# Weight loads, weight stores and phase loads issued in another order in a fused S4D and GLU kernel

## Chip, cores and metric

The kernel runs on one core of a Trainium2 chip. The metric is device time in microseconds (us). Beside the times there is one profiled execution of the kernel; its trace lists every instruction on the engines PE (TensorE), with PEld for its weight loads, DVE (VectorE), ACT (ScalarE), POOL (GpSimd) and SP (SyncE), which here does nothing but issue DMAs ("SPq" in the views).

## The reference

For a sequence of 2048 positions with D = 448 channels, the sum of three terms over a layer-normalised input:

```python
def _A_ref(u, log_A_real, A_imag, C_real, C_imag, log_dt, D_skip):
    ...
    P = jnp.exp((A * dt[:, None])[:, :, None] * pos[None, None, :])
    K = 2.0 * jnp.einsum("dn,dnl->dl", C, P).real
    ...
    y = jnp.fft.irfft(Uf * Kf[None, :, :], L2)[:, :, :L]
    ...
    return y + u * D_skip[None, None, :]
...
def _B_ref(x, w_gate, w_up, w_down):
    g = jnp.einsum("bsd,df->bsf", x, w_gate)
    u = jnp.einsum("bsd,df->bsf", x, w_up)
    h = _sigmoid(g) * u
    return jnp.einsum("bsf,fd->bsd", h, w_down)
...
return x + _A_ref(xn, ...) + _B_ref(xn, w_gate, w_up, w_down)
```

A is a long convolution whose kernel K is made of 256 complex exponentials a channel; B is a gated linear unit with F = 1792 inner columns.

## The kernel before

Everything is fp32, done on PE as products of split numbers: each operand is cast to fp32r (the high part) and the rest is kept as a low part, and a product is high x high + high x low + low x high.

**The GLU** (`glu()`) runs over two halves of the positions. In each half it takes 14 tiles of 128 inner columns, in groups of 3, 3, 3, 3 and 2. For a tile it gets wh and wl (high and low of w_gate and w_up; two buffers each), runs two gates (`gate`, the matmuls of line 687 into gu, then th on ACT, hf on DVE, and the split of hf into hh on ACT and hl on DVE), and gets dh and dl (high and low of w_down). After a group come the down products (line 794, po) and their sums on DVE (line 799, acc). In half 0 the raw weights are loaded by `w_load` (lines 621 and 623: per matrix one transfer of 192 KB and two of 32 KB, into wraw, one buffer) and `rd_load` (line 629), and split: wh on ACT (line 737), wl on DVE (line 741), dh on ACT (line 762), dl on POOL (line 763). Tiles 3 and 6 to 13 are not split again in half 1: wh, wl, dh and dl are stored to DRAM (wt_d at line 744, dt_d at line 766) right after they are made and read back in half 1 (line 752, 775). The loads of tiles 0 and 1 are issued at the start of the program.

**The convolution's kernel.** A preparation splits phases U, V and T of all channels into high and low parts and stores them to ph_d in DRAM (12 stores at lines 384 and 389). `kgen` then goes over 56 chunks of 8 channels. For each pair of chunks `phase_load` (line 470) brings the rows of ph_d into a tile ph (two of them) in nine transfers of 8 rows. For a chunk, PE multiplies ph with the constant sel (line 520, tr), ACT turns that into sines and cosines (S, lines 528 to 531), POOL raises magnitudes me and mf by products of powers pm (line 498), which DVE (line 435) and ACT (lines 433 and 438) made every eighth chunk in `powers`, DVE multiplies them (Et at lines 581 and 582, Ft at line 583), and PE forms 64 products a chunk in ko (line 595). Every fourth chunk ACT copies ko to ks (line 608) and PE takes it through the first stage of a Fourier transform (line 546, kp and kq). After the last chunk come spectra and inverse transforms.

**The order.** `glu` and `kgen` are generators; each `yield` tells how much PE work was issued, and a driver alternates between them by that. A scheduler then arranges the instructions of each engine once, when the program is built; on the chip each engine, and SP, works strictly in its own order, and a waiting instruction holds everything behind it on that engine. `tc.issue_after(x)` keeps an instruction behind x in that order, `hp` raises its priority.

Of the kernel before, what the change touches and what calls it, by code (L numbers as in the profile page):

```python
# [11 lines left out]
F32 = mybir.dt.float32  # L12
F32R = mybir.dt.float32r
I32 = mybir.dt.int32
AF = mybir.ActivationFunctionType
ALU = mybir.AluOpType
# [4 lines left out]
D = 448  # L21
N = 256
# [6 lines left out]
NFT = F // 128  # L29
# [9 lines left out]
CP = D // 4  # L39
# [8 lines left out]
DC = 8  # L48
# [7 lines left out]
def _tables():  # L56

    a = np.arange(NA)[:, None]
    k1 = np.arange(NK1)[None, :]
    ang = 2 * np.pi * ((a * k1) % 64) / 64.0  # L60


    wk = np.zeros((4, NA, 2, 2, 32))

    wx = np.zeros((4, NA, 64))
    for j in range(4):
        wk[j, :, 0, j % 2] = np.cos(ang)[:, :32]
        wk[j, :, 1, j % 2] = -np.sin(ang)[:, :32]
        wk[j, :, 1, j % 2, 0] = np.cos(ang)[:, 32]
        wx[j, :, :NK1] = np.cos(ang)  # L70
        wx[j, :, NK1:] = -np.sin(ang)[:, 1:32]
    b = np.arange(NB)[:, None]
    k2 = np.arange(64)[None, :]
    tab = np.zeros((NK1, 128, 128))
    bk = np.zeros((2, 2, 64, 2, 128))
    for q in range(NK1):
        al = 2 * np.pi * ((b * (q + 64 * k2)) % 4096) / 4096.0
        c, s = np.cos(al), np.sin(al)
        tab[q] = np.block([[c, -s], [s, c]])
        if q in (0, 32):  # L80


            for h in range(2):

                split = lambda t: t.reshape(64, 2, 32).transpose(0, 2, 1)
                both = lambda r, i: np.stack([split(r), split(i)], 3).reshape(64, 128)
                bk[q // 32, h, :, 0] = both(c.T, s.T)
                bk[q // 32, h, :, 1] = both(-s.T, c.T)

    tab[0, 64:] = 0.0  # L90
    t32 = np.concatenate([tab[32][:, None], bk[1].reshape(128, 2, 128)], 1)
    tab = tab[:32].reshape(8, 4, 128, 128).transpose(0, 2, 1, 3)

    wf = np.zeros((2, 2, 4, 8, 32, NA))
    for k in range(32):
        ang = 2 * np.pi * ((k * (64 * np.arange(NA)[None] + np.arange(64)[:, None])) % 4096) / 4096.0
        re = (1.0 if k == 0 else 2.0) / 4096.0 * np.cos(ang)
        im = -2.0 / 4096.0 * np.sin(ang)
        if k == 0:
            im = np.broadcast_to(np.cos(np.pi * np.arange(NA))[None] / 4096.0, im.shape)  # L100
        wf[:, 0, k % 4, k // 4] = re.reshape(2, 32, NA)
        wf[:, 1, k % 4, k // 4] = im.reshape(2, 32, NA)

    sel = np.zeros((128, 2, DC, 32))
    st = np.arange(32) + 0.5
    for e in range(DC):
        sel[[e, DC + 2 + e, 2 * DC + 2 + e], 0, e] = st, -st, -st  # L110
        sel[[64 + e, 66 + 2 * DC + e, 96 + e], 1, e] = st, -st, -st
        sel[[64 + DC + e, 96 + DC + e, 96 + 2 * DC + e], 1, e] = [[1.0], [-1.0], [-1.0]]
    for row, tb_ in ((DC, 0), (64 + 2 * DC, 1)):
        sel[row, tb_], sel[row + 1, tb_] = MAGIC, -MAGIC
    f = lambda v, s: np.ascontiguousarray(v.reshape(s).astype(np.float32))
    return {
        "c_wk": f(wk, (128, 2, 64)),
        "c_wx": f(wx, (128, 64)),
        "c_tab": f(tab, (8, 128, 4, 128)),
        "c_t32": f(t32, (128, 3, 128)),  # L120
        "c_bk": f(bk[0], (128, 2, 128)),
        "c_wf": f(wf, (128, 32, NA)),
        "c_sel": f(sel, (128, 512)),
        "c_id": np.eye(128, dtype=np.float32),
    }
# [3 lines left out]
def s4d_glu_kernel(ctx, tc, io):  # L129
    nc = tc.nc  # L130
# [5 lines left out]

    dram = ctx.enter_context(tc.tile_pool(name="dram", bufs=1, space=DRAM))
    acc_d = dram.tile([128, 8, D], F32, name="acc_d")
    ph_d = dram.tile([D, 6, N], F32, name="ph_d")
    x1_d = dram.tile([64, NB, D], F32, name="x1_d")  # L140
    sk_d = dram.tile([128, D // 32, 32, 32], F32, name="sk_d")
    wt_d = dram.tile([2, NFT, 128, 8 * 128], F32, name="wt_d")
# [188 lines left out]
    def prep(pool, h, srcs):  # L331
# [44 lines left out]
            v.tensor_scalar(part(fr, i), part(aim, i), 1.0 / TWO_PI, dt(i), ALU.mult, ALU.mult)  # L376
        nc.scalar.copy(ki, fr)
        U, V, T = aim, fr, w3
        rows = ph_d[2 * CP * h : 2 * CP * h + 2 * CP].rearrange("(t p) i n -> p t i n", t=2)

        def high(i, src):
            hi = slots[f"P{i}"][:, h]
            nc.scalar.copy(hi, src)
            nc.sync.dma_start(rows[:, :, 2 * i], three(hi).bitcast(F32))

        def low(i, src):
            lo = src.bitcast(F32R)
            nc.gpsimd.tensor_tensor(lo, src, slots[f"P{i}"][:, h], ALU.subtract)
            nc.sync.dma_start(rows[:, :, 2 * i + 1], three(lo).bitcast(F32))

        v.tensor_tensor(U, fr, ki, ALU.subtract)
        nc.scalar.activation(ki, U, AF.Identity, scale=64.0)
# [32 lines left out]
                ps[:, :, :CP].rearrange("p k (g e) -> p k g e", e=DC),  # L425
            )

    def powers(pms, g, behind=None):

        w = W1s[0][:, NCH * g : NCH * g + NCH].rearrange("p g h e -> p (g h e)")  # L430
        pm = pms[g % 2]
        with tc.issue_after(behind.ins) if behind else nullcontext():
            nc.scalar.activation(pm[:, 0], w, AF.Identity, bias=one)
        for j in (1, 2, 3, 4, 5, 7, 8, 9, 10, 11):
            v.scalar_tensor_tensor(pm[:, j], w, 2.0, w, ALU.add, ALU.mult)  # L435
            w = pm[:, j]
        for o in (slice(1, 6), slice(7, 12)):
            nc.scalar.activation(pm[:, o], pm[:, o], AF.Identity, bias=one)

    def kgen(pk):  # L440
        fts, mls, sins = [], [], []
# [13 lines left out]
        pms = [tl["pm0"]]  # L455
        nc.gpsimd.memset(pms[0][:, 6], 1.0)
        with hp(HP):
            powers(pms, 0)


        pht = [tl["ph0"], tl["ph1"]]
# [2 lines left out]

        def phase_load(b):
            t = pht[b % 2]
            src = ph_d[16 * b : 16 * b + 16].rearrange("(k r) c n -> c r k n", k=2)
            for r0, parts in ((0, [0]), (DC + 2, [0, 1]), (64, [2, 4]), (66 + 2 * DC, [2]), (96, [3, 4, 5])):
                for j, i in enumerate(parts):
                    nc.sync.dma_start(t[r0 + DC * j : r0 + DC * j + DC].bitcast(F32), src[i])  # L470

        mes = [tl["me0"], tl["me1"]]
        nc.gpsimd.memset(mes[0][:, :, 0:1], 1.0)
# [91 lines left out]
        for g in range(NCK // NCH):  # L565
            for c in range(NCH):
# [1 line left out]
                S = nxt  # L568
                me, mf = (m[:, 2 * DC * (c % 2) : 2 * DC * (c % 2) + 2 * DC] for m in mags)
                if c == 4 and NCH * (g + 1) < NCK:  # L570
                    with tc.issue_after(fts[0].ins):
                        powers(pms, g + 1, sins[0])
                if cn + 1 < NCK:
                    nxt = ahead(cn + 1)
                    if c % 2 == 1:
# [39 lines left out]
    def w_load(f, raw=None, eng=nc.sync):  # L615
        fs = slice(128 * f, 128 * f + 128)
        if raw is None:
            raw = pg.tile([128, 2, 4, 128], F32, name="wraw", bufs=1)
        for i, nm in enumerate(("B_w_gate", "B_w_up")):
            w = io[nm]  # L620
            eng.dma_start(raw[:, i, 0:3], w[0:384, fs].rearrange("(k p) f -> p k f", p=128))
            for h in range(2):
                eng.dma_start(raw[64 * h : 64 * h + 64, i, 3], w[384:448, fs])
        return raw
# [81 lines left out]
        to.append((hh, hl))  # L706

    def glu():
        for half in range(2):
            if half == 1:  # L710
                for q in (2, 3):
# [2 lines left out]
            for fs_ in ORDER[half]:  # L714
# [14 lines left out]
                for n_, (f, t) in enumerate(order):  # L729
                    if t == 0:  # L730
                        wh = pg.tile([128, 2, 4, 128], F32R, name="wh", bufs=2)
                        if half == 0:
                            first = len(raws) == 2
                            raw, rd = raws.pop() if raws else (w_load(f), None)
                            wl = w_low()
                            with hp(HP):
                                nc.scalar.copy(wh, raw)
                                if first:
                                    v.scalar_tensor_tensor(wl, raw, lim[:, 0, 0:1], wh, ALU.mult, ALU.subtract)
                                else:  # L740
                                    v.tensor_tensor(wl, raw, wh, ALU.subtract)  # L741
                            if f not in RAW:
                                for t_, d_ in kept((wh, wl), wt_d, f):
                                    nc.sync.dma_start(d_, t_)
                        elif f in RAW:
                            raw, wl = w_load(f, eng=nc.gpsimd), w_low()
                            nc.gpsimd.tensor_copy(wh, raw)
                            nc.gpsimd.tensor_tensor(wl, raw, wh, ALU.subtract)
                        else:
                            wl = w_low()  # L750
                            for t_, d_ in kept((wh, wl), wt_d, f):
                                nc.sync.dma_start(t_, d_)
                        ws.append((wh, wl))
                    between = (lambda s_=mid[n_]: step(*s_)) if cross and mid[n_] else None
                    yield from gate(ws[f - f0], xq[2 * half + t], hs[t], between)
                    if t == 0:
                        dh = pg.tile([128, D], F32R, name="dh", bufs=FCH[0])
                        if half == 0:
# [3 lines left out]
                                nc.scalar.copy(dh, rd)  # L762
                            nc.gpsimd.tensor_tensor(dl, rd, dh, ALU.subtract)  # L763
                            if f not in RAW:
                                for t_, d_ in kept((dh, dl), dt_d, f):
                                    nc.sync.dma_start(d_, t_)
                        elif f in RAW:
                            dl = d_low()
                            rd = rd_load(f, pg.tile([128, D], F32, name="rdw", tag="wraw", bufs=1), nc.gpsimd)
# [360 lines left out]
```

## Time and profile before

| | us |
|---|---|
| runs | 749.53, 754.44, 755.01 (median 754.44) |
| profiled execution | 757.44 |
| its span, first to last instruction | 755.5 |
| mean granted TensorE clock over the span | 0.957 |

About 1.9 us of the profiled execution lie outside the span. In the timeline a row is the start and the duration in us, engine, line, operation with output and inputs, the number of like instructions in the row and, in brackets, how long the engine was idle before it and what ended that. A view of windows has one row a stretch: the busy time (and number) of each engine, the granted clock as a share of full speed, the share of DMA time and GB/s. The waits of SP list what a DMA issue waited for: us in total, how often, and the longest.

### The profile page before, as it was taken

How to read it: one execution, taken by the hardware profiler on the slowest of the kernel's cores; microseconds unless marked ns; L12 is line 12 of the kernel's file. 1: busy time of each engine (PE TensorE's matmuls, PEld its weight loads, DVE VectorE, ACT ScalarE, POOL GpSimd, SP SyncE). 2: the span in 40 equal slices, each digit the busy share in tenths (PEclk: the TensorE clock that was granted, in tenths of full speed). 3: DMA queues.
4: the chain of work that ended last, by engine and by line, in shares of the span. 5: the costliest groups of instructions: out<-in, count | busy, mean ns of one | idle time of the engine just before them, and what ended most of it. 6: DMA issues, size and time to landing. Idle time of an engine off the chain costs nothing.

```text
span 755.5 us, 19270 instructions
## 1 busy us (share of the span) xinstructions
PE 691.4 (92%) x7780; PEld 540.6 (72%) x7780; DVE 564.4 (75%) x776; ACT 421.5 (56%) x650; POOL 363.9 (48%) x423
## 2 busy tenths in 40 slices
PE   2798799995997999888999999999999999998994
PEld 2675588874886778555678887887877787776783
DVE  5769997697889889879558978988875555664553
ACT  3635455666777776987377777867742222322310
POOL 2102017695697668675328686596754001341001
PEclk9988899997999899989799999999999999999998
DMA  9926327434412543445663333222169999999646
GB/s 207 220 70 195 103 77 228 133 113 147 145 45 98 176 150 113 133 135 154 182 200 116 100 111 126 97 95 75 43 159 246 268 240 235 244 251 245 162 130 163
DMA packets 92776, 115.86 MB, mean 153 GB/s; under 512 B 12560, under 2 KB 80656, under 8 KB 92432
## 3 DMA queue, kind: packets, MB, share of 16 engines
q1 hardware_dynamic: 83376, 94.16, 45.7%
q10 hardware_dynamic: 6736, 14.57, 6.3%
q0 software_dynamic: 2576, 5.90, 3.2%
q8 instruction: 61, 1.00, 0.6%
q14 instruction: 27, 0.22, 0.1%
HBM read 70.75 MB, written 43.84 MB: 152 GB/s over the span
## 4 chain that ended last, share of the span: by engine, by line
PE 52%; DVE 14%; POOL 12%; DMA 8%; issue 5%; ACT 5%; SPq 2%; ACTq 1%; POOLq 0%; DVEq 0%
PE gu L687 20%; PE po L794 13%; PE sp L876 6%; POOL me L498 6%; PE ko L595 5%; PE pv L903 3%; POOL mf L498 3%; PE tr L520 2%; DVE Ft L583 2%; DVE Et L582 2%; DVE Et L581 2%; DVE wl L741 1%; POOL dl L763 1%; DVE pm L435 1%; DVE hl L705 1%
## 5 line engine op out<-in xcount | busy, mean ns | idle before, releaser
L498 POOL TENSOR_TENSOR me<-me,pm 128x32 f32<-128x32 f32 (+1 forms) x168 | 141.5, 842 | 101.4 <-DVE Et L582 89.8
L498 POOL TENSOR_TENSOR mf<-mf,pm 128x64 f32<-128x64 f32 (+1 forms) x112 | 118.5, 1058 | 4.2
L687 PE MATMUL gu<-xh,wh 128*128 128x512 f32 x336 | 103.3, 415 | 4.1 <-ACT xh L216 4.1
L687 PE MATMUL gu<-xh,wl 128*128 128x512 f32 x336 | 97.7, 398 | 0.0
L687 PE MATMUL gu<-xl,wh 128*128 128x512 f32 x336 | 96.3, 393 | 0.0
L794 PE MATMUL po<-dh,hh 128*128 128x448 f32 x224 | 86.5, 386 | 6.3 <-DVE acc L799 3.4
L581 DVE TENSOR_TENSOR Et<-me,S 128x1024 f32<-128x1024 f32 x56 | 77.7, 1388 | 14.8 <-ACT S L531 12.3
L582 DVE TENSOR_TENSOR Et<-me,S 128x1024 f32<-128x1024 f32 x56 | 78.8, 1408 | 13.3 <-ACT me L511 10.0
L794 PE MATMUL po<-dl,hh 128*128 128x448 f32 x224 | 84.0, 375 | 0.0
L794 PE MATMUL po<-dh,hl 128*128 128x448 f32 x224 | 83.5, 374 | 0.0
L583 DVE TENSOR_TENSOR Ft<-mf,S 128x1024 f32<-128x1024 f32 x56 | 78.4, 1400 | 4.4 <-POOL mf L498 3.1
L687 PEld LDWEIGHTS gu<-xh,wh 128*128 128x128 f32 x336 | 63.8, 197 | 23.2 <-ACT xh L216 5.6
L528 ACT ACTIVATE S<-tr 128x1024 f32<-128x1024 f32 x56 | 57.8, 1032 | 39.2 <-PE tr L520 37.5
L595 PEld LDWEIGHTS ko<-Et,Ft 128*32 128x32 f32 x3584 | 56.0, 113 | 30.4 <-issue 14.6
L703 ACT CAST hh<-hf 128x512 fp32r<-128x512 f32 x56 | 35.0, 625 | 75.6 <-DVE hf L698 64.8
L687 PEld LDWEIGHTS gu<-xh,wl 128*128 128x128 f32 x336 | 64.4, 192 | 15.5 <-DVE pl L304 0.7
L595 PE MATMUL ko<-Et,Ft 128*32 128x64 f32 x3584 | 66.6, 226 | 9.7 <-DVE Ft L583 5.3
L698 DVE SCALAR_TENSOR_TENSOR hf<-th,gu 128x512 f32<-128x512 f32 x56 | 38.2, 681 | 48.4 <-PE gu L687 37.0
L687 PEld LDWEIGHTS gu<-xl,wh 128*128 128x128 f32 x336 | 63.6, 189 | 14.2 <-issue 0.7
L799 DVE SCALAR_TENSOR_TENSOR acc<-po,acc 128x448 f32<-128x448 f32 x80 | 48.1, 615 | 25.8 <-PE po L794 25.7
L531 ACT ACTIVATE S<-S,hpi 128x1024 f32<-128x1024 f32 x56 | 65.6, 1172 | 0.0
L695 ACT ACTIVATE th<-gu 128x512 f32<-128x512 f32 x56 | 33.6, 600 | 55.9 <-PE gu L687 48.0
(196 smaller groups left out, 1308.4 us busy)
## 6 DMA issues: line engine op xcount, KB each, us to landing
sk_d<-sk ACTq DMA_DIRECT2D x14, 512.0 KB
sx<-x_d SPq DMA_DIRECT2D x32, 224.0 KB
skl<-sk_d SPq DMA_DIRECT2D x16, 448.0 KB
vp<-v_d SPq DMA_DIRECT2D x16, 448.0 KB
v_d<-vt SPq DMA_DIRECT2D x62, 112.0 KB
wt_d<-wh SPq DMA_DIRECT2D x9, 512.0 KB
wt_d<-wl SPq DMA_DIRECT2D x9, 512.0 KB
wl<-wt_d SPq DMA_DIRECT2D x9, 512.0 KB
```

The source lines that it names most:

```text
L498: ins = nc.gpsimd.tensor_tensor(m[:, :, w + a : 2 * w : n], m[:, :, a:w:n], par(base + i).unsqueeze(2).to_broadcast([128, 4 * DC, w // n]) ...
L528: nc.scalar.activation(rows(cs), pv, AF.Abs)
L531: sins[:] = [nc.scalar.activation(cs, cs, AF.Sin, scale=-TWO_PI, bias=hpi)]
L581: v.tensor_tensor(Et[:, :, :, 32:64], two(me[:, :, 32:64]), S[:, 1::-1], ALU.mult)
L582: v.tensor_tensor(Et[:, :, :, 0:32], two(me[:, :, 0:32]), S[:, 1:3, :, ::-1], ALU.mult)
L583: fts[:] = [v.tensor_tensor(Ft, two(mf), S[:, 3:5], ALU.mult)]
L595: mm = nc.tensor.matmul(ko[32 * j : 32 * j + 32, sl], Ft[:, cc, DC * h + 4 * q + j], Et[:, cc, DC * h + 4 * q + j], start=(k == 0), stop=( ...
L687: glu_mm[:] = [nc.tensor.matmul(ps, a_, b_, start=(n == 0), stop=(n == len(mm) - 1))]
L698: marks[1] = v.scalar_tensor_tensor(hf, th, 1.0, pgu[1], ALU.add, ALU.mult)
L794: glu_mm[:] = [nc.tensor.matmul(po, a_[:, bs], w_, start=(n == 0), stop=(n == 3 * fc - 1))]
L799: v.scalar_tensor_tensor(acc[:, b], po, 0.5, acc[:, b], ALU.mult, ALU.add)
L876: mm = nc.tensor.matmul(to, tb[:kk, t, 64 * c : 64 * c + 64], rhs, start=True, stop=True, skip_group_check=True,)
```

## The change

Four edits:

- In half 0 the raw weights of the next tile are loaded (`w_load(f + 1)`) right behind the instructions that make wl of this tile, ahead of its gates; before, they were loaded when the next tile's turn came. wraw keeps its one buffer.
- The stores of wh, wl, dh and dl go onto a list; the list is issued after the next gate.
- ph_d becomes three DRAM tiles: phu_d (high and low of U), phv_d (high V, high T, low T, low V) and phh_d (high V and high T a second time). A pair of chunks is loaded in four transfers of 8, 16, 16 and 32 rows; the rows of sel are permuted to match. The preparation issues 16 stores where it issued 12.
- `powers` becomes a generator in four pieces, which its callers run through at once; each piece stands behind the same Ft.

```diff
@@ tables @@
-        sel[[e, DC + 2 + e, 2 * DC + 2 + e], 0, e] = st, -st, -st
-        sel[[64 + e, 66 + 2 * DC + e, 96 + e], 1, e] = st, -st, -st
-        sel[[64 + DC + e, 96 + DC + e, 96 + 2 * DC + e], 1, e] = [[1.0], [-1.0], [-1.0]]
+        sel[[e, DC + 2 + 2 * e, DC + 3 + 2 * e], 0, e] = st, -st, -st
+        sel[[64 + 2 * e, 96 + 4 * e, 99 + 4 * e], 1, e] = st, -st, -st
+        sel[[65 + 2 * e, 97 + 4 * e, 98 + 4 * e], 1, e] = [[1.0], [-1.0], [-1.0]]
@@ preparation of the phases @@
-        rows = ph_d[2 * CP * h : 2 * CP * h + 2 * CP].rearrange("(t p) i n -> p t i n", t=2)
+        def keep(d, i, src):
+            rows = d[2 * CP * h : 2 * CP * h + 2 * CP].rearrange("(t p) i n -> p t i n", t=2)
+            nc.sync.dma_start(rows[:, :, i], three(src).bitcast(F32))

         def high(i, src):
             hi = slots[f"P{i}"][:, h]
             nc.scalar.copy(hi, src)
-            nc.sync.dma_start(rows[:, :, 2 * i], three(hi).bitcast(F32))
+            keep((phu_d, phv_d, phv_d)[i], (0, 0, 1)[i], hi)
+            if i:
+                keep(phh_d, i - 1, hi)

         def low(i, src):
             ...
-            nc.sync.dma_start(rows[:, :, 2 * i + 1], three(lo).bitcast(F32))
+            keep((phu_d, phv_d, phv_d)[i], (1, 3, 2)[i], lo)
@@ phase_load @@
-            src = ph_d[16 * b : 16 * b + 16].rearrange("(k r) c n -> c r k n", k=2)
-            for r0, parts in ((0, [0]), (DC + 2, [0, 1]), (64, [2, 4]), (66 + 2 * DC, [2]), (96, [3, 4, 5])):
-                for j, i in enumerate(parts):
-                    nc.sync.dma_start(t[r0 + DC * j : r0 + DC * j + DC].bitcast(F32), src[i])
+            for r0, d, n in ((0, phu_d, 1), (DC + 2, phu_d, 2), (64, phh_d, 2), (96, phv_d, 4)):
+                src = d[16 * b : 16 * b + 16, :n].rearrange("(k r) i n -> (r i) k n", k=2)
+                nc.sync.dma_start(t[r0 : r0 + DC * n].bitcast(F32), src)
@@ glu @@
-                            raw, rd = raws.pop() if raws else (w_load(f), None)
+                            raw, rd = raws.pop()
                             ...
+                            if not raws and f + 1 < NFT:
+                                raws.append((w_load(f + 1), None))
                             if f not in RAW:
-                                for t_, d_ in kept((wh, wl), wt_d, f):
-                                    nc.sync.dma_start(d_, t_)
+                                stores.extend(kept((wh, wl), wt_d, f))
                         ...
                     yield from gate(ws[f - f0], xq[2 * half + t], hs[t], between)
+                    for t_, d_ in stores:
+                        nc.sync.dma_start(d_, t_)
+                    stores.clear()
                     if t == 0:
                         ...
                             if f not in RAW:
-                                for t_, d_ in kept((dh, dl), dt_d, f):
-                                    nc.sync.dma_start(d_, t_)
+                                stores.extend(kept((dh, dl), dt_d, f))
```

In `powers` each of the four pieces is wrapped in `tc.issue_after(fts[0].ins)` and followed by a `yield`; before, the call as a whole was.

More of the change, by code (lines that the diff above doesn't have):

```diff
@@ L138, in s4d_glu_kernel @@
     acc_d = dram.tile([128, 8, D], F32, name="acc_d")
-    ph_d = dram.tile([D, 6, N], F32, name="ph_d")
+    phu_d = dram.tile([D, 2, N], F32, name="phu_d")
+    phv_d = dram.tile([D, 4, N], F32, name="phv_d")
+    phh_d = dram.tile([D, 2, N], F32, name="phh_d")
     x1_d = dram.tile([64, NB, D], F32, name="x1_d")
@@ L426, in turn, with powers @@
             )
-    def powers(pms, g, behind=None):
+    def powers(pms, g, fts, behind=None):
         w = W1s[0][:, NCH * g : NCH * g + NCH].rearrange("p g h e -> p (g h e)")
@@ L433, in powers @@
             nc.scalar.activation(pm[:, 0], w, AF.Identity, bias=one)
[L434 to L438, printed above, removed]
+        for js, o in (((1, 2, 3), None), ((4, 5, 7), slice(1, 6)), ((8, 9), None), ((10, 11), slice(7, 12))):
+            with tc.issue_after(fts[0].ins) if behind else nullcontext():
+                for j in js:
+                    v.scalar_tensor_tensor(pm[:, j], w, 2.0, w, ALU.add, ALU.mult)
+                    w = pm[:, j]
+                if o:
+                    nc.scalar.activation(pm[:, o], pm[:, o], AF.Identity, bias=one)
+            yield
     def kgen(pk):
@@ L457, in kgen @@
         with hp(HP):
-            powers(pms, 0)
+            for _ in powers(pms, 0, None):
+                pass
         pht = [tl["ph0"], tl["ph1"]]
@@ L570, in kgen @@
                 if c == 4 and NCH * (g + 1) < NCK:
-                    with tc.issue_after(fts[0].ins):
-                        powers(pms, g + 1, sins[0])
+                    for _ in powers(pms, g + 1, fts, sins[0]):
+                        pass
                 if cn + 1 < NCK:
@@ L708, in glu @@
     def glu():
+        stores = []
         for half in range(2):
```

## The prediction

> **What bounds the kernel now.** I read the page first (busy shares, slices, the chain of waits), then the idle gaps of PE one by one in the timeline, and the granted clock in 4 us windows around each.
>
> ```profile
> span 755.5 us, 19270 instructions
> ...
> PE 691.4 (92%) x7780; PEld 540.6 (72%) x7780; DVE 564.4 (75%) x776; ACT 421.5 (56%) x650; POOL 363.9 (48%) x423
> ...
> PE   2798799995997999888999999999999999998994
> ...
> PEclk9988899997999899989799999999999999999998
> ...
> PE 52%; DVE 14%; POOL 12%; DMA 8%; issue 5%; ACT 5%; SPq 2%; ACTq 1%; POOLq 0%; DVEq 0%
> ```
>
> The first three rows are the span, the busy time of each engine and PE in 40 slices of 18.9 us; then the clock granted to PE, and the shares of the chain that ended last. PE is busy for 691.4 of 755.5 us, so only 64 us are idle, and the rest can shrink only where matmuls ran at less than full clock. The change doesn't touch the number of matmuls. The slices lose time only in the left half: from about slice 21 (390 us) PE is at 9 throughout until the end. The changed edits work up to there (their phase loads go on to the last chunk), so what they are worth is read from the gaps before 390 us. SP, which issues nearly all DMAs and does most of what is edited, carries 2% of the chain.
>
> **The raw weights a tile ahead.** The largest early gap is this one.
>
> ```profile
> 31.78 1.19 PE L687 MATMUL gu<-xh,wh 128*128 128x512 f32 x4 [0.60 <-ACT xh L216]
> ...
> 32.80 0.60 PE L207 MATMUL tr<-ident,xn 128*128 128x128 f32 x4
> ...
> 34.17 0.38 SPq L621 DMA_DIRECT2D wraw<-in_B_w_up_dram  x1
> 35.11 1.10 SPq L623 DMA_DIRECT2D wraw<-in_B_w_up_dram  x2
> 35.57 0.56 ACT L762 CAST dh<-rd 128x448 fp32r<-128x448 f32 x1 [2.37 <-DMA rd<-in_B_w_down_dram]
> 36.04 0.58 ACT L216 CAST xh<-tr 128x512 fp32r<-128x512 f32 x1
> ...
> 36.31 1.41 SPq L629 DMA_DIRECT2D rd<-in_B_w_down_dram  x2
> 36.68 1.22 PE L687 MATMUL gu<-xh,wh 128*128 128x512 f32 x2 [3.27 <-ACT xh L216]
> ```
>
> Each timeline row is start, duration, engine, line, operation, and in brackets the idle time before it and what ended it. The transposes of x end at 32.80 + 0.60 = 33.40, but ACT stands in its queue at the cast of w_down, waiting for a DMA, and only then makes xh; PE waits 3.27 us. In the changed program's instruction order ACT casts xh ahead of this dh, because w_load of the next tile is now issued right behind wl and stands on SP ahead of rd; the cast of dh comes later. So PE waits only for the cast, as it did at 31.78, where the gap was 0.60: 3.27 - 0.60 = 2.7 us less idle. What is late next is dh of this tile; its DMA moves behind a raw load, whose rows here are issued in 0.38 + 1.10 us, so I let it land some 3 us later, at about 38.5 (35.57 + 3). Its cast then delays nothing until PE has finished its gate.
>
> The gap has a second price, the clock.
>
> ```profile
> 32.00:36.00 4.00, 1.40 (x8) 0.94 (x7) 3.94 (x7) 1.63 (x4) 0.00 (x0) 0.96 0.89 193
> 36.00:40.00 4.00, 3.32 (x8) 2.65 (x9) 3.96 (x16) 0.62 (x2) 1.14 (x1) 0.50 0.51 149
> ```
> ```profile
> 34.00:48.00 14.00, 11.32 (x38) 0.76 0.25 68
> ```
> ```profile
> 100.00:114.00 14.00, 13.85 (x61) 1.00 0.31 88
> ```
> ```profile
> 36.68 10.74 PE gu L687 x34
> ...
> 47.50 0.61 ACT th L695
> ...
> 48.13 0.07 DVE hf L698
> ```
>
> The first two windows have the busy time of PE, PEld, DVE, ACT and POOL, then the clock: 0.96 before the gap, 0.50 after it. The next two give the gate's matmuls (L687) alone: 38 in 11.32 us at clock 0.76, 0.298 each, against 13.85 / 61 = 0.227 at 1.00. The gap thus costs 38 x 0.071 = 2.7 us more, if it is what lowers the clock. For that speaks a later gap and the windows behind it:
>
> ```profile
> 358.24 0.47 PE L794 MATMUL po<-dh,hh 128*128 128x448 f32 x1 [2.21 <-DVE xl L214]
> ```
> ```profile
> 246.00:250.00 4.00, 4.00 (x106) 3.18 (x97) 3.88 (x4) 2.48 (x4) 1.78 (x1) 0.50 0.63 190
> ...
> 360.00:364.00 4.00, 4.00 (x43) 2.02 (x44) 2.97 (x5) 1.87 (x4) 0.00 (x0) 0.50 0.50 194
> ```
>
> After 2.21 us of idle time PE ran at 0.50, while the 0.60 us at 31.78 left the clock up. I take the clock term as gained, since 0.60 is far below 2.21, and its loss as a rival. The Trainium skill, in "TensorE: Matmul & The Clock Gate" (section "Part 1: The HAM clock gate"), lets the clock fall to half after about one idle window of some 3.4 us that runs freely; by that rule 3.27 us needn't lower it, something else may have, and the gain would be the idle time alone; the drop after 2.21 us doesn't agree with its figure.
>
> The chain of waits holds 34 of these matmuls, then th and hf; from then on DVE splits weights and prepares phases:
>
> ```profile
> 50.00:75.00 25.00, 22.14 (x108) 14.56 (x107) 24.74 (x41) 13.16 (x20) 4.08 (x1) 0.86 0.65 183
> ```
>
> It is busy for 24.74 of 25 us. A DVE without idle time moves as a whole: 2.7 + 2.7 = 5.4 us earlier. Its bounds are 0 (dh's cast, in order on ACT, holds the next th as long as it held xh) and 5.4.
>
> For later tiles the early call does little: raw has one buffer, so its load waits for wl of the tile before in both programs, and the order on SP shows these loads hoisted already.
>
> **The deferred stores, and the second large gap.**
>
> ```profile
> 171.21 1.20 POOL L763 TENSOR_TENSOR dl<-rd,dh 128x448 fp32r<-128x448 f32 x1
> ...
> 172.43 0.34 SPq L766 DMA_DIRECT2D dt_d<-dl  x1
> ...
> 174.63 1.66 SPq L623 DMA_DIRECT2D wraw<-in_B_w_up_dram  x2
> ...
> 178.01 1.04 ACT L737 CAST wh<-wraw 128x1024 fp32r<-128x1024 f32 x1 [5.95 <-DMA wraw<-in_B_w_up_dram]
> ...
> 182.81 0.56 ACT L608 COPY ks<-ko 128x512 f32<-128x512 f32 x1
> ...
> 183.42 0.37 PE L546 MATMUL kp<-wk,ks 64*64 64x64 f32 x1 [7.89 <-ACT ks L608]
> ```
> ```profile
> 184.00:188.00 4.00, 3.06 (x119) 2.90 (x112) 2.80 (x4) 4.00 (x6) 0.00 (x0) 0.50 0.37 109
> ```
>
> POOL delivers dl late, SP stands at its store with the rest of the next raw load queued behind it, ACT stands at wh waiting for that load, and ks, which PE needs, stands behind wh on ACT. The gap is 7.89 us, and at half clock the 3.06 us of the next window hold 1.5 us of excess. This is what deferring stores could cure. In the changed program's order, however, dl's store of this tile again comes before the second half of the raw load, POOL's order up to this dl is the same, and the nine phase loads before the store become four, while SP waits there anyway. So I cost the deferral at nothing here. Bounds: -9.4 (7.89 + 1.5) if the store does move out of the way, +1.4 if all of the later gate's stores wait: four at the 0.34 of the row.
>
> **The phases.** Preparing them issues 16 stores instead of 12, and the weight store passed by them moves; the rows of this place:
>
> ```profile
> 126.51 0.54 SPq L384 DMA_DIRECT2D ph_d<-P  x1
> ...
> 128.37 2.02 SPq L389 DMA_DIRECT2D ph_d<-w  x1
> ...
> 130.43 1.12 SPq L623 DMA_DIRECT2D wraw<-in_B_w_up_dram  x2
> ...
> 133.43 1.05 ACT L737 CAST wh<-wraw 128x1024 fp32r<-128x1024 f32 x1 [5.21 <-DMA ph<-ph_d]
> ```
>
> The last phase store stands ahead of a raw load on SP, and ACT waits for that at wh. Two of the four added stores come in this stretch, and 2 x 0.54 = 1.1 us is the upper bound, 0 the lower (the copies fit into SP's earlier waits); I take 0.8, as the last stores are the ones that count.
>
> ```profile
> 183.70 3.23 SPq L470 DMA_DIRECT2D ph<-ph_d  x9
> ```
> ```profile
> SPq L470 <- PE tr L520: 82.5, 16, 10.7
> ```
>
> The nine loads of a pair take SP 3.23 us, 0.36 each. Four instead of nine, in 28 pairs, is 140 x 0.36 = 50 us of SP. The second row says why this isn't 50 us of the kernel: SP waits 82.5 us in these loads for PE to release the tile, so they are mostly early. Only where a pair is late, as behind 128.37 above and at a few later pairs, are 5 x 0.36 = 1.8 us on the path; I take 0.8, about half of one such saving, between 0 and, for five late pairs, 5 x 1.8 = 9 us.
>
> powers keeps its instructions and its place behind the same Ft; DVE and ACT execute the same, at nothing.
>
> **The reordering.** The instructions of 195 to 390 us are arranged anew: the chunk work stands earlier against the gates (in the changed program PE comes to the twentieth chunk's ko after some 25 half-tiles of gate instead of 26). There PE now waits for products of DVE:
>
> ```profile
> 245.42 1.93 PE L595 MATMUL ko<-Et,Ft 128*32 128x64 f32 x64 [3.28 <-DVE Et L581]
> ```
>
> Transposes that come earlier feed ACT and DVE earlier, which helps; ko that comes earlier meets Et and Ft sooner, which hurts. Such a wait is 3.28 us and then, in the window from 246 shown above, 4.00 busy us at half clock, thus 2.0 more: 5.3. One of them more or less is the bound on my forecast; I take 0.
>
> Sum: -5.4 + 0.8 - 0.8 + 0 = -5.4 us. The profiled run took 757.44 us with a span of 755.5, 3.0 us (0.4%) over the median of 754.44; a difference of a few us carries over unscaled, so 754.4 - 5.4 = 749 us.
>
> **The rivals.** *Late weights cured as well.* The store leaves the way at 172 and the gap of 7.89 goes, or earlier transposes end one or two of DVE's waits: 749 - 9.4 = 740, with a wait of 5.3 more 734. For it: store and load stand in one queue, and both are moved. Against: POOL, not SP, is late at 171.21, and the order of the stores is the same.
>
> *The early gain is lost or halved.* If the clock falls at 36 us whatever the gap, only 2.7 us of idle time go: 752. If raw is not ahead (one buffer, a hoisted load) or dh holds ACT as before, nothing goes: 754. For it: ACT takes its work in order, and PE is idle elsewhere in its first two slices too (2 and 7 tenths busy). Against: the drop stands right behind the gap. The rule of the Trainium skill's "TensorE: Matmul & The Clock Gate" named above would give 752 here.
>
> *PE comes too early.* In order on PE, ko of chunks 12 to 25 moves ahead of gates that used to fill the time in which DVE and POOL make Et and Ft. Each chunk at which PE arrives more than some 2 us before the product costs 5.3; from the second on the early gain is gone; three make 749 + 16 = 765. For it:
>
> ```profile
> 225.00:250.00 25.00, 21.08 (x319) 16.71 (x317) 23.35 (x26) 17.69 (x27) 17.24 (x18) 0.88 0.32 107
> ```
>
> DVE has 23.35 of 25 us busy there, so it can't deliver sooner. Against: gates not done earlier remain to be done later, and PE's total is the same.
>
> **How the numbers follow.** Forecast 0.42, own range 744 to 754 (one wait of 5.3 either way); cured as well 0.27, 734 to 745; lost or halved 0.09, 752 to 755; PE too early 0.22, 757 to 770. About 1%, 7.5 us, is what a measurement here tells from no change. Faster than 746.9 are the second case and a quarter of the first: 0.27 + 0.10 = 0.37. Slower than 762 are four fifths of the last: 0.18. The rest is 0.45. The range leaves out the far ends of the second and the fourth case, about 0.1 each: 737 to 765.
>
> **What would show it.** In the new profile the gate near 34 us starts some 0.6 us after its transposes, with the clock at 1.00 until 44, and th follows at about 42 instead of 47.50; a gap over 2 us there, or half clock, refutes the first term. The wait of wh on the raw load and a gap of 7 to 8 us at ks should still stand near 173 to 178; if it is gone, the first rival holds. Phase loads appear as four issues of about 0.36. Waits before ko between 195 and 390 us should sum to what they are now within 5 us; three new ones over 2 us with windows at 0.50 make the slower rival right.

## The result, and the profile after

| | before | after |
|---|---|---|
| median of 15 runs, us | 754.45 | 748.48 |
| lowest and highest, us | 749.53, 761.67 | 743.47, 753.66 |
| profiled execution, span, us | 755.5 | 749.6 |
| its mean granted clock | 0.957 | 0.964 |

The ratio after to before is 0.9918 (95% interval 0.9889 to 0.9947): 6.2 us less. The ratios, here and below, leave out executions that took over 1.5% longer than the fastest of the same kernel, and the medians don't; the two differ where several are left out, four of twelve in e2 and four of eleven in e10. The forecast was 749, with 737 to 765 as its range, and the likeliest class, within 1%.

The page of the kernel after, the same rows as before:

```profile
span 749.6 us, 19094 instructions
...
PE 687.9 (92%) x7780; PEld 539.4 (72%) x7780; DVE 565.6 (75%) x776; ACT 421.9 (56%) x650; POOL 388.3 (52%) x423
...
PE   2897899996997999999989999999999999987994
...
PEclk9998899998999899979999999999999999999998
```

PE's busy time is 3.5 us less with the same number of matmuls, which goes with the higher clock. The rest of the difference in span, 2.4 us, is idle time. Where it went shows when the same work is followed through both traces. The starts of like instructions, in us:

| | before | after | difference |
|---|---|---|---|
| th of the second gate | 29.36 | 28.58 | -0.8 |
| th of the third gate | 47.50 | 41.43 | -6.1 |
| th of the twelfth gate | 123.88 | 118.09 | -5.8 |
| first copy ks | 182.81 | 175.90 | -6.9 |
| eighth copy ks | 397.72 | 389.73 | -8.0 |
| a th in the spectra | 667.21 | 658.49 | -8.7 |
| two th later | 696.92 | 691.24 | -5.7 |

Less the 0.8 us by which this execution was ahead from the start, 5.3 us come from one place, the third gate. Nothing is gained from there to the twelfth; about one more has come by the first copy ks, one by the eighth, and three are lost again near 680 us. The first place, in the timeline of the kernel after:

```profile
30.98 1.20 PE L696 MATMUL gu<-xh,wh 128*128 128x512 f32 x4 [1.27 <-ACT xh L218]
...
32.02 0.60 PE L209 MATMUL tr<-ident,xn 128*128 128x128 f32 x4
...
32.65 0.59 ACT L218 CAST xh<-tr 128x512 fp32r<-128x512 f32 x1 [0.24 <-PE tr L209]
...
33.29 0.74 PE L696 MATMUL gu<-xh,wh 128*128 128x512 f32 x2 [0.68 <-ACT xh L218]
...
37.60 0.57 ACT L776 CAST dh<-rd 128x448 fp32r<-128x448 f32 x1 [4.36 <-DMA rd<-in_B_w_down_dram]
...
41.43 0.60 ACT L704 ACTIVATE th<-gu 128x512 f32<-128x512 f32 x1 [3.26 <-PE gu L696]
```

ACT makes xh as soon as the transposes end, and only then stands at dh, 4.36 us for its DMA; nobody needs dh yet. The gap of PE is 0.68 instead of 3.27 us, and the windows of this kernel (busy time of PE, PEld, DVE, ACT and POOL, clock, DMA share, GB/s) show full clock where before stood 0.50:

```profile
32.00:36.00 4.00, 3.32 (x17) 2.57 (x16) 3.94 (x8) 0.99 (x2) 0.00 (x0) 1.00 1.09 228
36.00:40.00 4.00, 4.00 (x19) 3.34 (x18) 3.86 (x17) 0.57 (x1) 1.15 (x1) 1.00 0.35 88
40.00:44.00 4.00, 4.00 (x22) 2.50 (x22) 3.14 (x13) 2.57 (x5) 0.00 (x0) 1.00 0.22 57
```

The second large gap is still there, shorter:

```profile
164.61 2.13 POOL L777 TENSOR_TENSOR dl<-rd,dh 128x448 fp32r<-128x448 f32 x1
...
166.77 0.34 SPq L768 DMA_DIRECT2D dt_d<-dl  x1
...
168.32 1.14 SPq L632 DMA_DIRECT2D wraw<-in_B_w_up_dram  x2
...
171.49 1.05 ACT L747 CAST wh<-wraw 128x1024 fp32r<-128x1024 f32 x1 [3.20 <-DMA wraw<-in_B_w_up_dram]
...
175.90 0.56 ACT L617 COPY ks<-ko 128x512 f32<-128x512 f32 x1
...
176.51 0.27 PE L555 MATMUL kp<-wk,ks 64*64 64x64 f32 x1 [4.26 <-ACT ks L617]
...
179.47 1.94 PE L604 MATMUL ko<-Et,Ft 128*32 128x64 f32 x64 [1.78 <-DVE Et L590]
```

It is the chain of before, link by link: POOL's dl, its store on SP, the raw load behind the store, wh behind the load, ks behind wh. In the kernel before the first ko behind this stall waited too:

```profile
186.34 1.94 PE L595 MATMUL ko<-Et,Ft 128*32 128x64 f32 x64 [0.94 <-DVE Et L581]
```

And two waits of PE are new:

```profile
131.89 0.80 PE L529 MATMUL tr<-sel,ph 128*128 128x512 f32 x2 [2.03 <-DMA ph<-phv_d]
...
387.75 1.42 PE L604 MATMUL ko<-Et,Ft 128*32 128x64 f32 x64 [2.00 <-DVE Ft L592]
```

So PE's gaps before the work on ks (kp) and the first ko after it fell from 7.89 + 0.94 to 4.26 + 1.78, but 2.03 of that had moved to 131.89: all gaps of PE over 0.25 us from 115 to 195 us sum to 9.7 us before and 8.1 after. That DVE and POOL set the pace there, so that PE only waits at another place, is argued and not shown; they are busy for 24.79 and 23.90 of the 25 us from 150 on.

The loss near 680 us is in work that none of the edits touch. First the kernel before, then the kernel after:

```profile
678.00 4.56 ACTq L235 DMA_DIRECT2D out_dram<-ac  x3
682.60 0.62 ACT L703 CAST hh<-hf 128x512 fp32r<-128x512 f32 x1 [10.73 <-DMA out_dram<-ac]
...
684.19 0.98 PE L876 MATMUL sp<-skl,tb 128*64 128x224 f32 x8 [0.94 <-ACT vt L909]
```
```profile
670.75 0.69 DVE L707 SCALAR_TENSOR_TENSOR hf<-th,gu 128x512 f32<-128x512 f32 x1 [1.32 <-PE gu L696]
...
674.40 4.58 ACTq L237 DMA_DIRECT2D out_dram<-ac  x3
...
679.02 0.62 ACT L712 CAST hh<-hf 128x512 fp32r<-128x512 f32 x1 [15.87 <-DMA out_dram<-ac]
...
680.62 0.98 PE L889 MATMUL sp<-skl,tb 128*64 128x224 f32 x8 [4.03 <-ACT vt L922]
```

Three stores of the output stand on ACT in both kernels, with hh, th and vt behind them. Their 4.58 us are not the price of issuing. One by one the three issues start at 674.40, 675.51 and 678.66 us and take 0.36, 0.36 and 0.32; in between ACT stands, and by the trace's semaphores it stands until earlier DMAs have landed (of v_d before the first two, of sx before the third). Nor is this time what changed, 4.56 us before. What changed is its start: hf, which hh needs, ended 3.0 us before the first issue (at 671.44), where in the kernel before it ended as that issue began (at 678.10). PE idles 4.03 us where it idled 0.94 before.

### The profile page after: what moved, and what is told of

The parts are those of the page before. It is cut to its first block, busy times and chain, and to the rows that moved or that the text cites. A ratio compares the mean times of both kernels' runs of the same rounds, so it can differ in the third digit from the quotient of the medians.

```text
span 749.6 us, 19094 instructions
## 1 busy us (share of the span) xinstructions
PE 687.9 (92%) x7780; PEld 539.4 (72%) x7780; DVE 565.6 (75%) x776; ACT 421.9 (56%) x650; POOL 388.3 (52%) x423
## 4 chain that ended last, share of the span: by engine, by line
PE 42%; DMA 7%; DVE 3%; ACT 2%; issue 1%; ACTq 1%; POOL 1%; SPq 0%; POOLq 0%; DVEq 0%
PE gu L696 15%; PE po L807 10%; PE sp L889 5%; PE ko L604 4%; PE pv L916 3%; PE tr L529 2%; DMA sx<-x_d 1%; DMA tb<-in_c_tab_dram 1%; DMA v_d<-vt 1%; DMA vp<-v_d 1%; DMA acc_d<-acc 1%; PE kp L555 1%; DMA out_dram<-ac 1%; ACTq L681 1%; PE pv L951 1%
## 5 line engine op out<-in xcount | busy, mean ns | idle before, releaser
L507 POOL TENSOR_TENSOR me<-me,pm 128x32 f32<-128x32 f32 (+1 forms) x168 | 147.2, 876 | 85.2 <-DVE Et L591 72.6
L507 POOL TENSOR_TENSOR mf<-mf,pm 128x64 f32<-128x64 f32 (+1 forms) x112 | 128.5, 1147 | 5.3
L696 PE MATMUL gu<-xh,wl 128*128 128x512 f32 x336 | 97.4, 396 | 0.0
L590 DVE TENSOR_TENSOR Et<-me,S 128x1024 f32<-128x1024 f32 x56 | 81.7, 1459 | 11.7 <-ACT S L540 11.1
L591 DVE TENSOR_TENSOR Et<-me,S 128x1024 f32<-128x1024 f32 x56 | 79.7, 1424 | 11.4 <-ACT me L520 9.0
L696 PEld LDWEIGHTS gu<-xh,wh 128*128 128x128 f32 x336 | 61.9, 192 | 21.1 <-issue 5.1
L714 DVE TENSOR_TENSOR hl<-hf,hh 128x512 fp32r<-128x512 f32 x56 | 50.2, 896 | 18.5 <-ACT hh L712 18.5
```

What stands on the lines that cost most here:

```text
L507: ins = nc.gpsimd.tensor_tensor(m[:, :, w + a : 2 * w : n], m[:, :, a:w:n], par(base + i).unsqueeze(2).to_broadcast([128, 4 * DC, w // n]) ...
L590: v.tensor_tensor(Et[:, :, :, 32:64], two(me[:, :, 32:64]), S[:, 1::-1], ALU.mult)
L591: v.tensor_tensor(Et[:, :, :, 0:32], two(me[:, :, 0:32]), S[:, 1:3, :, ::-1], ALU.mult)
L696: glu_mm[:] = [nc.tensor.matmul(ps, a_, b_, start=(n == 0), stop=(n == len(mm) - 1))]
L714: v.tensor_tensor(hl, hf, hh, ALU.subtract)
```

## The experiments

What stands in a kernel's text and what its engines do are two things here. In the built program the deferral of the stores alone gives the kernel before the very same order on all engines, SP included; so does the new `powers`; and taking either out of the changed kernel leaves its order as it is. Wherever the text calls for a store, the scheduler put it at the same place. These two edits did nothing, and the kernels that follow leave them out, but for those made from the changed kernel itself (e5 and e11). What remains are the loads ahead and the four transfers.

**The swap of two casts on ACT** (e1, repeated as e6). In the kernel before, dh of tile 1 is put behind the cast xh:

```diff
-                nc.scalar.copy(xh[:, k, o], p)
+                cast = nc.scalar.copy(xh[:, k, o], p)
+                if k == 1:
+                    turned[:] = [cast]
...
-                            with hp(HP), tc.issue_after((act if f == 1 else marks)[0].ins):
+                            with hp(HP), tc.issue_after((turned if f == 1 else marks)[0].ins):
                                 nc.scalar.copy(dh, rd)
```

> The kernel before, with one thing changed: on ACT the cast dh of tile 1 stands behind the last of the three casts xh it used to stand ahead of. All loads and stores stay in their order on SP. My theory (the early gap is ACT standing at dh, and the half clock is the gap's doing): the gap of 3.27 us before the third gate falls to about 0.7, the clock stays at 1.00 from 36 to 44 us, th follows at about 42 instead of 47.5, and the kernel takes 749 us, ratio 0.993. Rival (the clock falls there anyway): only 2.7 us of idle time go, 752, and the window from 36 to 40 still shows 0.50. Rival (the load ahead itself is needed): the swap alone gives under 1 us.

> The swap of dh and xh on ACT alone once more, since the profile of the first run of it was 6 us above its median: 747 to 749 us, the gap before the third gate 0.7, its clock 1.00 unless the gap before the second gate is over 2 us.

Measured: 747.70 us, ratio 0.9899 (0.9865 to 0.9934), and again 745.72, 0.9886 (0.9848 to 0.9924). It isn't one thing that changed, though. Up to some 330 us the engines keep the order of the kernel before, but for these two casts and two or three other instructions; from there on the scheduler has exchanged instructions on PE, ACT, DVE and POOL, though the edit touches nothing there. The stretch from the fifth copy ks to the eighth, 302 to 398 us in the kernel before, takes 91.7, 92.0 and 91.5 us in e2, e3 and e6, which have this order there, and 95.6 and 94.4 in the kernel before and in e8, which have PE's old one. So the 8 us gained are probably not the third gate's alone. (e1, e7 and e10 have the new order on PE too and take 97.4 to 98.2 us; the last section says why.)

The profiled execution of the first took 755.82 us, far above its median, and is the more telling for it. The timeline of e1:

```profile
32.68 1.54 PE L689 MATMUL gu<-xh,wh 128*128 128x512 f32 x4 [3.20 <-ACT xh L216]
...
35.75 1.22 PE L689 MATMUL gu<-xh,wh 128*128 128x512 f32 x2 [0.67 <-ACT xh L216]
```

and its windows:

```profile
32.00:36.00 4.00, 2.65 (x9) 1.86 (x10) 3.81 (x8) 2.69 (x6) 0.00 (x0) 0.67 1.05 190
36.00:40.00 4.00, 4.00 (x10) 3.17 (x11) 4.00 (x8) 0.57 (x1) 1.14 (x1) 0.50 0.47 119
344.00:348.00 4.00, 4.00 (x72) 2.05 (x71) 4.00 (x6) 2.96 (x6) 0.00 (x0) 0.50 0.22 52
348.00:352.00 4.00, 4.00 (x14) 1.06 (x10) 2.83 (x5) 0.53 (x1) 3.17 (x7) 0.50 0.39 87
```

The gap before the third gate is gone as forecast (0.67), but in this execution the one before the second gate is 3.20 us where it was 0.60, and the clock falls there instead. That gap scatters: over the thirteen traces of this study it is between under 0.6 and 3.33 us. In the three with 2.16 or more the windows from 32 to 36 show a clock of 0.63 to 0.67; in the ten with 1.80 or less the clock stays at 0.96 or more until the third gate. So the same place shows thirteen times how the clock follows the gap, with the step between 1.80 and 2.16 us. The step holds for this place only: in the kernel after PE idles 2.61 us before 665.90 and the windows from 664 to 672 show 1.00, and it idles 1.04 us before 325.54 and the window from 328 shows 0.50. The later rows show half clock with PE busy throughout; of that below.

**Loads ahead, only the first and all of them** (e2 and e3, in this order).

```diff
+                            if f == 1:
+                                raws.append((w_load(f + 1), None))
```
```diff
-                            raw, rd = raws.pop() if raws else (w_load(f), None)
+                            raw, rd = raws.pop()
...
+                            if not raws and f + 1 < NFT:
+                                raws.append((w_load(f + 1), None))
```

> The kernel before, with only the raw load of tile 2 issued right behind wl of tile 1; ACT, DVE, POOL and PE get the same order as with the swap alone, SP has the load ahead of w_down of tile 1 and two constants. My theory: same as the swap, 749 us, since the load only matters by the order it gives ACT. Rival (the earlier load also makes wh of tile 2 earlier): 1 to 2 us less than the swap.

> The kernel before, with every raw load a tile ahead, stores and phases as before. My theory: later loads were hoisted already, so as the swap, 749 us within 1. Rival (loads ahead also shorten the stall at the copy ks of the first four chunks, 7.9 us before, 4.3 after the change): 745 or less, and the gap before kp near 176 us is about 4.

Measured: e2 750.25 us, 0.9904 (0.9873 to 0.9935); e3 747.72, 0.9902 (0.9873 to 0.9931). Both the same as the swap, which moves no raw load at all. In e3's trace th of the third gate comes 5.3 us earlier against the second (41.93 - 29.11 against 47.50 - 29.36). The load ahead matters because with it the scheduler puts the cast of tile 1's w_down behind xh; anything else is too small for intervals of 0.3%. The rival of e3 is half there: the stall at ks has gaps of 2.57 + 3.84 us instead of 7.89 + 0.94, but a new one of 2.24 stands at 129.59, and the time shows nothing of it.

**Four transfers alone** (e4): the loads, the preparation's stores and sel as in the changed kernel, the rest as before.

> The kernel before, with only the phases in four transfers a pair and the 16 stores of the preparation. My theory by the comparison of the two traces (8.0 us ahead at 390 us, 5.8 of them from the early gap): 2 us less than before, 752 to 753, the gap of 3.27 at 36.7 us unchanged, and a new gap of about 2 us before the first tr. Rival (the rearranged order is worth nothing): 754 to 755. Rival (phases are what made the gain from 126 us on, by shortening the stall at ks from 7.9 to 4.3): 749 to 750.

Measured: 757.80 us, ratio 1.0038 (1.0011 to 1.0066). Slower, which none of the three expectations had; nor is the new gap before the first tr in its trace. The timeline of e4:

```profile
170.33 1.15 POOL L768 TENSOR_TENSOR dl<-rd,dh 128x448 fp32r<-128x448 f32 x1
...
171.50 0.34 SPq L771 DMA_DIRECT2D dt_d<-dl  x1
...
174.66 1.12 SPq L628 DMA_DIRECT2D wraw<-in_B_w_up_dram  x2
...
177.60 1.05 ACT L742 CAST wh<-wraw 128x1024 fp32r<-128x1024 f32 x1 [13.77 <-DMA wraw<-in_B_w_up_dram]
...
181.54 1.22 PE L525 MATMUL tr<-sel,ph 128*128 128x512 f32 x2 [9.48 <-ACT S L535]
...
186.36 0.36 PE L551 MATMUL kp<-wk,ks 64*64 64x64 f32 x1 [3.60 <-ACT ks L613]
```

In the order that belongs to the four transfers wh stands on ACT ahead of the chunk's S, so S, and PE's tr behind it, wait for the store of dl as well: 9.48 + 3.60 us of idle PE against 7.89 + 0.94 before.

**Stores that really are deferred** (e5, e8, e9, e10). The stores of dh and dl are held behind a later raw load by an explicit order; in the changed kernel:

```diff
                                 raws.append((w_load(f + 1), None))
+                            for t_, d_ in late:
+                                with tc.issue_after(lastld[0].ins):
+                                    nc.sync.dma_start(d_, t_)
+                            late.clear()
...
-                                stores.extend(kept((dh, dl), dt_d, f))
+                                late.extend(kept((dh, dl), dt_d, f))
```

Only two places on SP's queue change by it, and nothing on the engines.

> The changed kernel with the stores of dh and dl held back on SP behind the next tile's raw load, so that they really are deferred; PE, ACT, DVE and POOL keep the order of the changed kernel, and on SP only the stores of tiles 7 and 8 change places with parts of two raw loads. My theory (in the stall at ks, 4.26 us in the changed kernel, ACT waits 3.20 us at wh for a raw load that stands behind the store of dl): wh comes about 3 us earlier, the gap before kp falls to 1 to 2 us, and the kernel takes 745, ratio to before 0.987. Rival (DVE and POOL, busy for 24.8 and 23.9 of the 25 us before, set the end anyway): wh is early, but the gap moves to the next ko, its sum with the one before kp stays at 6 us, and the time stays at 748.

Measured: 743.23 us, ratio 0.9856 (0.9820 to 0.9892), against 0.9918 for the changed kernel. Its timeline:

```profile
166.18 1.05 ACT L750 CAST wh<-wraw 128x1024 fp32r<-128x1024 f32 x1
...
170.78 1.21 DVE L754 TENSOR_TENSOR wl<-wraw,wh 128x1024 fp32r<-128x1024 f32 x1
...
173.10 0.83 ACT L446 ACTIVATE pm<-pm,one 128x640 f32<-128x640 f32 x1 [2.85 <-DVE pm L443]
...
173.83 0.57 ACT L617 COPY ks<-ko 128x512 f32<-128x512 f32 x1
...
174.45 0.27 PE L555 MATMUL kp<-wk,ks 64*64 64x64 f32 x1 [4.18 <-ACT ks L617]
...
176.53 1.93 PE L604 MATMUL ko<-Et,Ft 128*32 128x64 f32 x64 [1.14 <-DVE Et L590]
```

wh no longer waits, but the gap before kp is as long as it was: ks now stands behind pm, which waits for DVE. So the stall took on a new releaser, as the rival had it; yet everything up to it is earlier. Against th of the second gate, ks comes at 173.83 - 29.69 = 144.1 us instead of 175.90 - 28.58 = 147.3. In the trace of e11 below, which has the same late stores, it comes at 176.87 - 29.52 = 147.35 again, so how the gain of 0.6%, whose two intervals just meet, comes about stays open.

> The kernel before, with only the stores of dh and dl held back behind a raw load two tiles on; PE keeps its order, ACT, DVE and POOL but for one to three places. Theory (the store of dl holds the raw load, and that holds wh and ks): wh of the tenth tile no longer waits 5.95 us for its load, and the kernel is 3 to 5 us faster, 750 to 751, ratio 0.994 to 0.996; the gap before kp may stay long, as in the changed kernel with late stores. Rival (the gain seen there was the earlier wh only in that rearranged order, or run to run scatter): 754 to 755.

> The phases in four transfers alone, with the stores of dh and dl held back in the same way; the order on ACT and POOL is that of the four transfers alone. Theory (the four transfers alone lost 0.4% because wh stood 13.8 us on ACT behind that store and raw load, with S and tr behind it): the gap of 9.5 us before tr shrinks by 4 us or more and the ratio falls from 1.004 to 0.996 or less. Rival (they lose elsewhere, in the rearranged order or by the four added stores): 1.002 to 1.005 again.

> The swap of dh and xh on ACT and the late stores, without the four transfers. If the two gains add: 0.990 x 0.995 = 0.985, 743. If the four transfers help once the stores are late, it stays behind the changed kernel with late stores (0.9856) by 0.3% or more.

Measured: e8 753.40 us, 0.9985 (0.9956 to 1.0014), no difference that can be told from none, so the 3 to 5 us of its theory are missing; e9 750.20, 0.9963 (0.9930 to 0.9995), where the four transfers alone had 1.0038; e10 0.9862 (0.9821 to 0.9903), which can't be told from the swap alone (0.9899 and 0.9886); the median of its eleven executions, 749.05 us, is well above the 743 expected. In e9 wh waits 3.67 us instead of 13.77, and the wait of tr for S is gone:

```profile
180.29 0.36 PE L551 MATMUL kp<-wk,ks 64*64 64x64 f32 x1 [5.55 <-ACT ks L613]
...
184.11 1.93 PE L600 MATMUL ko<-Et,Ft 128*32 128x64 f32 x64 [2.05 <-DVE Ft L588]
```

The loss of the four transfers was the store that holds the raw load: the interval of e9 lies wholly below that of e4. With it out of the way they are worth 0.9963 against 0.9985 for the late stores alone, a difference inside the intervals; nor can e10, which has no four transfers, be told from e5, which has them.

**Output stores off ACT** (e7, e11).

```diff
-            eng = (nc.sync, nc.scalar, nc.gpsimd)[outs[0] % 3]
+            eng = (nc.sync, nc.gpsimd)[outs[0] % 2]
```

> Loads ahead alone (stores and phases as before), and the stores of the output issued by SP and POOL in turn instead of SP, ACT and POOL. In the kernels seen so far ACT spends 4.6 us issuing three of them near 675 us, hh stands 10 to 16 us behind them, and PE then idles 1 to 4 us before sp. Theory (this issue is on the path): that gap falls under 1 us and the time is 745, 2 to 3 us under the loads ahead alone. Rival (SP, with more to issue, delays the loads of the spectra by as much): 748.

> The changed kernel with late stores of dh and dl, and the output stores issued by SP and POOL in turn. Theory (ACT's 4.6 us of issuing is on the path in some executions): 741 to 742, ratio 0.983, no gap over 1.5 us before sp near 675. Rival: 743, as without it.

Measured: e7 744.89 us, 0.9885 (0.9839 to 0.9930), beside 0.9902 for the same kernel with the output stores as before; e11 745.17, 0.9843 (0.9811 to 0.9874), beside 0.9856. In e7 hh no longer waits for the issue:

```profile
673.77 0.62 ACT L703 CAST hh<-hf 128x512 fp32r<-128x512 f32 x1 [6.27 <-DVE hf L698]
...
677.15 0.98 PE L878 MATMUL sp<-skl,tb 128*64 128x224 f32 x8
```

PE's gap before sp is gone in both, as it should be if the stores on ACT are what holds it. Since the kernels that keep these stores on ACT idle there for 0.9 to 4.1 us in some executions and less in others, a gain of a little over 1 us is likely, but inside the intervals; it isn't settled. e11 has the lowest ratio of all, 11 to 12 us under the kernel before and below the changed kernel's interval; against e5 it is open.

## Why the prediction was right

- **The raw weights ahead, -5.4.** Right in mechanism and size. 2.6 of idle time and the rest in clock, 5.3 us in the trace. As whole kernels the swap and both forms of the load give 0.989 to 0.990, some 8 us with an interval of 5 to 11, but that includes the stretch from the fifth copy ks to the eighth, some 3 us shorter in their order, so it doesn't say that the term was too small. That the load is needed was not claimed, and the swap shows that it isn't. The clock term, taken against the rival that half clock comes anyway, held in the changed kernel and in e3, e5, e7, e10 and e11; in e1, e2 and e6 the earlier gap brought half clock back.
- **The deferred stores, 0.** Right, and for the reason given: they aren't deferred. The sign that went with it, a gap of 7 to 8 us at ks, didn't come; it was 4.26 us, with 2.03 at another place. What a real deferral is worth was put at up to 9.4 by taking the whole gap and its clock. That was too much: with the store out of the way (e5) the gap stays and waits for DVE, and 4.7 us are gained (0.9918 to 0.9856, with intervals that just meet), in the kernel before no more than 3.3 (the end of e8's interval).
- **The phases, +0.8 - 0.8.** This is the step that failed. The added stores cost nothing to be seen: the end of the preparation keeps the lead of the third gate (132.63 us before, 126.95 after, at the first memset of me, 5.7 us). The saved issues gained nothing to be seen either. They were put at 50 us of SP, and SP's waits for PE in these loads, 82.5 us before, grew by 24:

```profile
SPq L479 <- PE tr L529: 106.5, 20, 11.9
```

  But with the order that belongs to them the four transfers cost 2.9 us alone (0.8 to 5.0), because wh came ahead of S behind the late load. The prediction had said of that very store that SP waits there anyway, and had not asked what stands on ACT behind wh in the new order.
- **The reordering, 0.** About -1 in the trace, from the first copy ks to the eighth. PE's gaps over 0.25 us before ko from 195 to 390 us sum to 7.9 us before and 7.8 after; that they stay within 5 us was the prediction's sign. The rival of PE coming too early was right that new waits arise (2.00 at 387.75, with a clock of 0.57 behind it), wrong that they add up: others shrank (the kernel before waits 3.10 at 332.27, the kernel after no more than 1.04 before any ko from 243 to 387).
- **The sum.** -5.4 against -6.2. As whole kernels the loads ahead gained 7.4 us (e3) where the sum has 5.4, and the four transfers lost 2.9 (e4) where it has nothing; together that is 4.5, and the intervals allow 6.2. That the forecast hit to a microsecond is in part luck, since a gain in the rearranged order and the loss of the transfers took each other away. The slices of the page were also read as full from 390 us on, where slice 37 (680 to 699 us) shows 8; there three of the microseconds won were lost again in the trace.

## What to carry to other kernels

Before costing an edit, see whether it changes the order that runs: two of the four edits here changed no engine's order. On an engine that works in order, look for an instruction that waits for a DMA and is needed late, with one behind it that is needed at once; exchanging the two was worth 5.3 us in the trace, and merging transfers alone cost 2.9. A store that waits for a slow producer should not stand ahead of a load in the same queue: it cost most where work that PE needed stood behind the load (e4 against e9), and nothing that could be measured in the kernel before (e8). A wait that is removed is worth only the time to the next one behind it. And a small edit to a program that is scheduled as a whole can rearrange work far away from it.

## What the runs showed that was not expected

Half clock lasts beyond the gap that brings it. In e1 it stood at 0.50 for 20 us from 344 on, with PE busy for all of the time (two of the windows are above); e7 and e10 show the same stretch, about 340 to 360, the kernel before only 360 to 370, e3 and e6 none there, but 10 us from about 326 on. The gaps ahead of it are 0.6 to 1.2 us in e1, e7 and e10, no longer than in executions that kept the clock (1.43 in e6), so a gap's length alone doesn't decide there. Its price can be read from the copies ks, since these kernels have the same order on PE there: from the fifth to the eighth e1, e7 and e10 take 97.4 to 98.2 us, e2, e3 and e6 91.5 to 92.0. Some 6 us is as much as the whole change is worth; it may go far to explain why single executions of one kernel scatter by 10 us, and it is why a profiled execution's span must not be compared alone. What decides it stays open; PE does small matmuls there as well (ko, with 32 rows of output each), but no run separated that.
